# Row scatters, gate columns and one small addition around the hand-over from attention to experts: which engine does what, and what waits for what

## The chip, the core and the metric

The kernel runs on one core of a Trainium2 chip. The metric is the device time of one execution in microseconds (us). The core has a matrix engine (TensorE, PE in the rows; PEld are its weight loads), a vector engine (VectorE, DVE), a scalar engine (ScalarE, ACT), GpSimd (POOL) and a queue engine (SyncE, SP). Each runs its own list of instructions in order, and they wait for each other by semaphores. Indirect DMAs (gathers and scatters by row number) are issued by POOL.

## What is computed

Chunked attention (8 batches, 8 heads, 576 positions, chunks of 64), and behind it a mixture of experts on its 4608 output rows: each row goes to the one expert of 8 with the largest logit.

```python
attn = softmax(q_c @ k_c^T / 8)          # per chunk of 64
x = (attn @ v_c) as rows [4608, 512]
logits = x @ w_gate                      # [4608, 8]
gate = max softmax probability (sum + 1e-9); e = argmax
out[row] = gate * (relu(x @ w1[e]) @ w2[e])
```

## The kernel before

The 4608 rows are 36 tiles of 128. The main loop (L1067 on) takes two tiles at a time, 18 rounds `g`: PE makes the scores of round `g` (L251) into the PSUM pair `psS`, DVE takes the maxima and differences (`mx` L266, `ex` L269), ACT the exponentials (L274), PE transposes (L297) and multiplies with v (L306), DVE writes the normalised rows into a ring of blocks `xb` of four tiles each (L318), PE transposes the rows (L329) and forms the logits (L341). The scores of the next round go into the same `psS`, so PE has to wait there until DVE's `ex` of the round before has read it.

The rows are routed in batches of 6, 6, 6, 6, 4, 4, 2, 2 tiles (called batches 0 to 7 below) by a generator `route`, whose steps are dealt out between the steps of the rounds by hand: `small_op(n)` deals n DVE steps, `advance("a")` an ACT step, and so on. The whole order on PE, DVE, ACT and POOL is written out this way. The steps of `route` that matter here: `gs` is the sum of the exponentials (L411), 1e-9 is added to it (L413), its reciprocal is the gate in column 0 of the small tile `ft` (L415), column 1 of `ft` is the row's number (written by POOL, L362); `di` is the row's place in the sorted order (L424); POOL then copies the two columns of `ft` into columns 512 and 513 of the rows in `xb` (L426). `lo` (L386) is one of the small DVE steps before these, with both of its inputs in SBUF.

`store(n)` (L442) then issues the indirect scatters of n tiles from `xb` to the DRAM table `xd`, one for each tile, on POOL. With `after` given, ACT first copies a value into a spare column of the tile (L445, a "mark"), so that the scatter can't be issued before the thing it was copied from exists. Expert slot 0 needs the first 18 tiles alone (`TE[0]` is 18): `gather(0)` fetches its 256 rows from `xd` after those are stored, on POOL (L600), in the middle of the main loop. Later scatters write to the same table, and waited for these two gathers.

While the last rounds run, ACT splits the first expert's weights into a high part (`whi`, casts L89), and POOL subtracts for the low part (`wlo`, TENSOR_TENSOR L90, 16 of them, both inputs in SBUF).

After the loop comes the hand-over ("the tail" below, L1114 to L1187): PE transposes slot 0's rows (L625), ACT and DVE split them into `xhl` (L627, L628), and PE fills the rest with pieces of slot 0's matrix products (`filler`, L674 and L767 to L769), while the last batches are routed and stored; then DVE computes the tables of places, and `gather(1)` fetches slot 1's rows, once every scatter has landed. From there on PE runs one expert slot after the other until the end.

Of the kernel before, what the change touches and what calls it, by code (L numbers as in the profile page):

```python
# [8 lines left out]
F32 = mybir.dt.float32  # L9
# [3 lines left out]
AF = mybir.ActivationFunctionType  # L13
ALU = mybir.AluOpType
# [4 lines left out]
P = 128  # L19
NT = 4608  # L20
D = 512
# [5 lines left out]
RB = 4  # L27
# [3 lines left out]
NMAX = max(BATCHES)  # L31
# [19 lines left out]
def attn_moe_kernel(ctx: ExitStack, tc: tile.TileContext, q, k, v, wg, w, w0, out):  # L51
    nc = tc.nc
# [7 lines left out]
    q, k, v = (a[:, :, 0:G * D].rearrange("g p (i x) -> g p i x", i=G) for a in (q, k, v))  # L60
# [70 lines left out]
    sm = c1.enter_context(tc.tile_pool(name="sm", bufs=2))  # L131
# [28 lines left out]
    TE = [first[i] for i in EARLY]  # L160
# [185 lines left out]
    def route(b, pl):  # L346


        t0, n = first[b], BATCHES[b]
        S3 = [P, n, E]  # L350

        xts = [(i, G, xb[(t0 + i) // RB % XB], (t0 + i) % RB) for i in range(0, n, G)]
        vec = nc.vector

        def small(name, dt=F32, k=E):
            return sm.tile([P, NMAX, k], dt, name=name, bufs=2)[:, 0:n, :]

        def flat(x):
            return x.rearrange("p t o -> p (t o)")

        ft = sm.tile([P, NMAX, 2], F32, name="ft", bufs=2)[:, 0:n, :]
        nc.gpsimd.tensor_copy(ft[:, :, 1:2], pid[:, t0:t0 + n].unsqueeze(2))  # L362
        yield "c"
        lg = small("lg")
# [45 lines left out]
        gs = small("gs", k=1)  # L410
        vec.tensor_reduce(flat(gs), eg, AX.X, ALU.add)  # L411
        yield "v"
        vec.tensor_scalar(gs, gs, 1e-9, None, ALU.add)  # L413
        yield "v"
        vec.reciprocal(ft[:, :, 0:1], gs)  # L415
        yield "v"
# [5 lines left out]
        di = small("di", I32, 1)  # L422
        with nc.allow_low_precision("whole numbers"):
            vec.tensor_reduce(flat(di), dst, AX.X, ALU.add)  # L424
        for i, m, x, r in xts:
            nc.gpsimd.tensor_copy(x[:, r:r + m, D:D + 2], ft[:, i:i + m, :])  # L426
        waiting.extend((b, i, t0 + i, di) for i in range(n))
        yield "a"
# [2 lines left out]
        if b + 1 in EARLY:  # L431
            g = early(EARLY.index(b + 1))
            active.append([g, next(g), True])
        if b == NBAT - 1:
            g = tables()
            active.append([g, next(g), True])

    waiting = []

    def store(n, after=None):  # L440

        for k, (b, i, t, di) in enumerate(waiting[:n]):  # L442
            x = xb[t // RB % XB][:, t % RB, :]
            if k == 0 and after is not None:
                nc.scalar.copy(x[:, XW - 1:XW], after)  # L445
            stored.add(t)
            nc.gpsimd.indirect_dma_start(  # L447
                out=xds[b % 2 * NMAX + i],
                out_offset=bass.IndirectOffsetOnAxis(ap=di[:, i, :], axis=0),
                in_=x, in_offset=None, bounds_check=NT - 1, oob_is_err=False)  # L450
        del waiting[:n]

    active = []
# [133 lines left out]
    def rows_of(u):  # L587
        return xg[0] if u in (0, 2) else xg[1]
# [8 lines left out]

    def rows_in(t, u, h):
        rows = TE[u] * P if u < 2 and h < 2 else NT
        nc.gpsimd.indirect_dma_start(  # L600
            out=t[:, :], out_offset=None, in_=xd[0:rows, :],
            in_offset=bass.IndirectOffsetOnAxis(ap=place(u, h)[0:t.shape[0], :], axis=0),
            bounds_check=rows - 1, oob_is_err=False)

    def gather(u):
        for h in range(2):
            rows_in(rows_of(u)[h], u, h)

    def gather_x(u):
        rows_in(xg3, u, 2)  # L610
# [104 lines left out]
    lo_, h0 = [], []  # L715
# [305 lines left out]
    st_e, st_l, st_x = {}, {}, {}  # L1021
# [92 lines left out]
    g = NG - 1  # L1114
# [19 lines left out]
    for h in range(2):  # L1134
        ids(0, rows_of(0)[h], h)

    store(2, px[0][:, 0:1])
    filler(2)
    ri = soft_d(su)
    x_out(g, px, ri, xb[g * G // RB % XB])  # L1140
    logits(g - 1)
    store(2, st_l[g - 1][:, 0:1])
    filler(1)
    advance("t")
    small_op(5)
    advance("a")
    filler(1)
    st_x[g] = x_t(g, xb[g * G // RB % XB])
    store(2, st_x[g][:, 0, 0:1])
    sel_(g - 1)  # L1150
    advance("c")
    filler(2)
# [1 line left out]
    small_op(7)  # L1154
    advance("a")
    logits(g)
    store(2, st_l[g][:, 0:1])
    filler(1)
    advance("t")
    sel_(g)  # L1160
# [2 lines left out]
    advance("a")  # L1163
    pauses()
    filler(2)
    store(2, h0[-1][0][:, 0:1].bitcast(F32))
    pauses()
    small_op(7)
    advance("a")
# [6 lines left out]
    while active:  # L1176
        for x in "cat":
            advance(x)
        small_op(2)
        pauses()  # L1180
        side_op(3)
        if halves[0] > 5:
            filler(1)
        if h0:
            store(2, h0[-1][0][:, 0:1].bitcast(F32))
    store(NMAX)
    assert len(stored) == NTILE  # L1187
    gather(1)
# [204 lines left out]
```

## Time and profile before

| | us |
|---|---|
| median of 3 runs (range) | 573.17 (572.85 to 578.56) |
| the profiled execution | 576.16 |
| its span, first to last instruction | 574.3 |
| PE busy in it | 556.0 |
| DVE busy in it | 426.1 |

The profiled execution is one of the same kernel, 3.0 us above the median. Where stretches are named below, they are us from the start of its span: the main loop runs to about 114, the tail to about 150, the expert slots to the end.

### The profile page before, as it was taken

To read this page: it belongs to the slowest core of one execution; us is meant where nothing else is said; L and a number is where in the kernel's file an instruction comes from. 1 tells how busy PE (TensorE), PEld (TensorE's weight loads), DVE (VectorE), ACT (ScalarE), POOL (GpSimd) and SP (SyncE) were. 2 spreads that over 40 slices of the span, in tenths; PEclk is the share of its full clock that TensorE was granted. 3 is DMA by queue.
4 is the path that set the end of the run, shared out by engine and by line. 5 is a ranking of instruction groups with operands and counts; after the bars stand their busy time and mean duration, and the time that the engine had idled before them with its cause. 6 is when DMAs were issued, how large, how long until landed. Compare 5 with 4: busy or idle time off the path is not lost.

```text
span 574.3 us, 13260 instructions
## 1 busy us (share of the span) xinstructions
PE 556.0 (97%) x4858; PEld 489.8 (85%) x4858; DVE 426.1 (74%) x840; ACT 281.8 (49%) x548; POOL 270.3 (47%) x293
## 2 busy tenths in 40 slices
PE   7999999979999999999999999999998999999995
PEld 6788888878898888999898898888988888899894
DVE  8899999976695878776787588645665765588775
ACT  1667766743244464554654454424443542356553
POOL 6025743387643655525473574523514252274352
PEclk9999999989999999999999999999998999999998
DMA  8999999435584453456145636644622652232021
GB/s 267 406 394 352 370 356 365 156 143 199 158 323 141 142 189 91 139 190 215 47 144 166 205 93 207 227 139 136 210 63 82 203 178 94 60 104 80 19 62 38
DMA packets 49038, 102.70 MB, mean 179 GB/s; under 512 B 14176, under 2 KB 28512, under 8 KB 45312
## 3 DMA queue, kind: packets, MB, share of 16 engines
q0 software_dynamic: 19776, 61.14, 31.2%
q1 hardware_dynamic: 29120, 39.88, 20.6%
q8 instruction: 63, 1.03, 0.8%
q14 instruction: 79, 0.65, 0.4%
HBM read 113.75 MB, written 19.56 MB: 232 GB/s over the span
## 4 chain that ended last, share of the span: by engine, by line
PE 57%; issue 10%; DMA 6%; POOL 3%; DVE 2%; POOLq 0%; ACT 0%; DVEq 0%
PE psS L674 11%; PE psS L681 11%; DMA xg<-xd,idx 5%; PE psV L767 4%; PE psV L769 4%; PE psV L768 4%; PE psU L769 4%; PE psU L768 4%; PE psU L767 4%; PE psL L681 3%; PE psL L674 3%; POOL xg L600 1%; POOL raw L573 1%; PE psK L785 1%; PE psK L787 1%
## 5 line engine op out<-in xcount | busy, mean ns | idle before, releaser
L83 DVE TENSOR_TENSOR wlo<-raw,whi 128x1024 fp32r<-128x1024 f32 x118 | 142.3, 1216 | 17.7 <-ACT whi L82 17.4
L82 ACT CAST whi<-raw 128x1024 fp32r<-128x1024 f32 x118 | 121.9, 1046 | 2.8 <-DMA raw<-in_w,widx 2.8
L701 ACT ACTIVATE hh<-psS 128x256 fp32r<-128x256 f32 x98 | 37.7, 384 | 158.0 <-PE psS L674 83.1
L573 POOL DMA_INDIRECT raw<-in_w,widx x62 | 70.0, 1129 | 93.9 <-DVE wlo L83 63.7
L799 POOL DMA_INDIRECT out_y<-y,oid x40 | 51.7, 1293 | 110.0 <-issue 28.3
L674 PE MATMUL psS<-xhl,whi 128*128 128x256 f32 x496 | 93.6, 288 | 3.2 <-DVE xhl L628 2.9
L600 POOL DMA_INDIRECT xg<-xd,idx x68 | 79.8, 1173 | 27.3 <-issue 17.3
L674 PEld LDWEIGHTS psS<-xhl,whi 128*128 128x128 f32 x496 | 81.4, 195 | 7.6 <-issue 4.2
L706 DVE SCALAR_TENSOR_TENSOR hl<-psS,hh 128x256 fp32r<-128x256 f32 x98 | 41.1, 421 | 59.2 <-ACT xx L685 37.8
L674 PE MATMUL psS<-xhl,wlo 128*128 128x256 f32 x248 | 71.1, 286 | 0.0
L681 PE MATMUL psS<-xhl,whi 128*128 128x320 f32 (+2 forms) x288 | 59.8, 333 | 0.5 <-ACT xhl L665 0.5
L681 PEld LDWEIGHTS psS<-xhl,whi 128*128 128x128 f32 x288 | 49.6, 188 | 4.6 <-ACT xhl L665 0.6
L767 PE MATMUL psV<-whi,hh 128*128 128x512 f32 x128 | 51.1, 399 | 2.3 <-issue 2.3
L769 PE MATMUL psU<-whi,hl 128*128 128x512 f32 x128 | 50.2, 392 | 0.3 <-DVE hl L706 0.3
L767 PE MATMUL psU<-whi,hh 128*128 128x512 f32 x128 | 50.4, 394 | 0.0
L768 PE MATMUL psU<-wlo,hh 128*128 128x512 f32 x128 | 50.4, 393 | 0.0
L768 PE MATMUL psV<-wlo,hh 128*128 128x512 f32 x128 | 50.1, 391 | 0.0
L769 PE MATMUL psV<-whi,hl 128*128 128x512 f32 x128 | 50.1, 391 | 0.0
L674 PEld LDWEIGHTS psS<-xhl,wlo 128*128 128x128 f32 x248 | 48.4, 195 | 0.0
L447 POOL DMA_INDIRECT xd<-xb,di x32 | 31.6, 988 | 17.4 <-issue 10.6
L90 POOL TENSOR_TENSOR wlo<-raw,whi 128x512 fp32r<-128x512 f32 x16 | 20.2, 1276 | 40.9 <-DMA spare<-in_k 23.8
L767 PEld LDWEIGHTS psV<-whi,hh 128*128 128x128 f32 x128 | 24.1, 188 | 8.6 <-issue 3.1
(257 smaller groups left out, 1151.7 us busy)
## 6 DMA issues: line engine op xcount, KB each, us to landing
qt<-in_q SPq DMA_DIRECT2D x17, 512.0 KB
xg<-xg SPq DMA_DIRECT2D x224, 32.0 KB
vb<-in_v SPq DMA_DIRECT2D x12, 512.0 KB
kb<-in_k SPq DMA_DIRECT2D x22, 256.0 KB
raw<-in_w SPq DMA_DIRECT2D x16, 256.0 KB
spare<-in_k SPq DMA_DIRECT2D x12, 256.0 KB
spare<-in_v SPq DMA_DIRECT2D x6, 512.0 KB
xg<-xd,idx POOLq DMA_INDIRECT x68, 3.6
```

The costliest lines, as they stand in the source:

```text
L82: nc.scalar.copy(hi, src)
L83: nc.vector.tensor_tensor(lo, src, hi.bitcast(F32), ALU.subtract)
L573: nc.gpsimd.indirect_dma_start(out=raw[c][:, :], out_offset=None, in_=w, in_offset=bass.IndirectOffsetOnAxis(ap=widx[:, u, c:c + 1], axis= ...
L600: nc.gpsimd.indirect_dma_start(out=t[:, :], out_offset=None, in_=xd[0:rows, :], in_offset=bass.IndirectOffsetOnAxis(ap=place(u, h)[0:t.sha ...
L674: nc.tensor.matmul(ph, a, b[:, kc, 0:BLK], start=kc + i == 0, stop=kc + i == 5)
L681: nc.tensor.matmul(ph, a[par][kc][:, f * 128:(f + 1) * 128], b[:, kc, 0:BLK + n], start=kc + i == 0, stop=kc + i == 5)
L701: nc.scalar.activation(hh, ph, AF.Relu)
L706: nc.vector.scalar_tensor_tensor(hl, ph, 0.0, hh.bitcast(F32), ALU.max, ALU.subtract)
L767: nc.tensor.matmul(py, hh, wh, start=f == 0, stop=False)
L768: nc.tensor.matmul(py, hh, wl, start=False, stop=False)
L769: nc.tensor.matmul(py, hl, wh, start=False, stop=f == 7)
L799: nc.gpsimd.indirect_dma_start(out=outs[m], out_offset=bass.IndirectOffsetOnAxis(ap=oid[u % 3][0:n, m:m + 1], axis=0), in_=y, in_offset=No ...
```

## The change

Five edits, which belong to the same part of the program. Below the changed lines the line numbers rise, by 4 to 8 (L413 becomes L417 and L628 becomes L636).

1. The row numbers `di` get four buffers in place of two.
2. Batches whose tiles lie in one block of `xb` (batches 4 to 7) have no `ft`: POOL writes the row number, and DVE the gate, straight into the rows; the copies by POOL (L426) fall away for them.
3. The addition of 1e-9 to `gs` moves from DVE (TENSOR_SCALAR) to ACT (an ACTIVATE with a bias), for all eight batches.
4. Scatters of tiles from 18 on are declared independent of slot 0's two gathers.
5. The stores of the tail have no mark any more.

```diff
         def small(name, dt=F32, k=E):
-            return sm.tile([P, NMAX, k], dt, name=name, bufs=2)[:, 0:n, :]
+            return sm.tile([P, NMAX, k], dt, name=name, bufs=4 if name == "di" else 2)[:, 0:n, :]
...
-        ft = sm.tile([P, NMAX, 2], F32, name="ft", bufs=2)[:, 0:n, :]
+        whole = t0 % RB + n <= RB
+        if whole:
+            ft = xts[0][2][:, t0 % RB:t0 % RB + n, D:D + 2]
+        else:
+            ft = sm.tile([P, NMAX, 2], F32, name="ft", bufs=2)[:, 0:n, :]
         nc.gpsimd.tensor_copy(ft[:, :, 1:2], pid[:, t0:t0 + n].unsqueeze(2))
...
-        vec.tensor_scalar(gs, gs, 1e-9, None, ALU.add)
+        nc.scalar.activation(flat(gs), flat(gs), AF.Copy, bias=1e-9)
         yield "v"
         vec.reciprocal(ft[:, :, 0:1], gs)
...
-        for i, m, x, r in xts:
+        for i, m, x, r in () if whole else xts:
             nc.gpsimd.tensor_copy(x[:, r:r + m, D:D + 2], ft[:, i:i + m, :])
...
-            nc.gpsimd.indirect_dma_start(
+            put = nc.gpsimd.indirect_dma_start(
...
+            if t >= TE[0]:
+                for got in fetched:
+                    tc.declare_no_dep(put.ins, got.ins, reason="rows from TE[0] * P on, and rows in front of them")
...
     def gather(u):
-        for h in range(2):
-            rows_in(rows_of(u)[h], u, h)
+        got = [rows_in(rows_of(u)[h], u, h) for h in range(2)]
+        if u == 0:
+            fetched.extend(got)
...
-    store(2, px[0][:, 0:1])
+    store(2)
...
-    store(2, st_x[g][:, 0, 0:1])
+    store(2)
...
-        if h0:
-            store(2, h0[-1][0][:, 0:1].bitcast(F32))
+        store(2)
```

(Three more stores of the tail lose their mark in the same way.)

On ACT in the main loop, at batch 1 (the batch whose `gs` DVE sums at 64.66 in the profile), the list read, with what each row waits for in brackets:

```order
L274 ACTIVATE ex<-ex 128x1024 [waits DVE_49]
L89 CAST whi_4_73<-raw_67 128x512 [waits DMAHW3_49]
L89 CAST whi_4_73<-raw_67 128x512 [waits DMAHW4_49]
L1040 COPY lp<-psL 128x256 [waits PE_49]
L429 ACTIVATE cb<-psK 128x8 [waits DVE_49]
```

and it reads now:

```order
L274 ACTIVATE ex<-ex 128x1024 [waits DVE_49]
L89 CAST whi_4_73<-raw_67 128x512 [waits DMAHW3_49]
L89 CAST whi_4_73<-raw_67 128x512 [waits DMAHW4_49]
L417 ACTIVATE gs<-gs 128x6 [waits DVE_49]
L1048 COPY lp<-psL 128x256 [waits PE_49]
L433 ACTIVATE cb<-psK 128x8 [waits DVE_49]
```

The addition stands behind the round's exponentials and behind two weight casts. At batch 0 it stands behind one cast, at batch 2 behind none, at batch 3 behind one, and each time behind the exponentials. DVE has nothing between `gs` and the reciprocal in these four batches, so its reciprocal waits for this row.

On DVE at the start of the tail (batch 4), before:

```order
L411 TENSOR_REDUCE gs<-eg 128x4
L413 TENSOR_SCALAR gs<-gs 128x4 [waits DVE_49]
L628 TENSOR_TENSOR xhl<-psS,xhl 128x4x128 [waits DMAHW6_49,DMAHW7_49,DMAHW5_49,Activation_49]
L628 TENSOR_TENSOR xhl<-psS,xhl 128x4x128 [waits Activation_49]
L415 RECIPROCAL ft<-gs 128x4 [waits DVE_49,Pool_49]
L419 TENSOR_TENSOR dst<-psK,oh_b 128x32
L424 TENSOR_REDUCE di<-dst 128x4 [waits DMASW6_49,DMASW1_49,DMASW7_49,DMASW0_49,DVE_49]
```

and now:

```order
L415 TENSOR_REDUCE gs<-eg 128x4
L636 TENSOR_TENSOR xhl<-psS,xhl 128x4x128 [waits DMAHW6_49,DMAHW7_49,DMAHW5_49,Activation_49]
L636 TENSOR_TENSOR xhl<-psS,xhl 128x4x128 [waits Activation_49]
L419 RECIPROCAL xb_124<-gs 128x4
L423 TENSOR_TENSOR dst<-psK,oh_b 128x32
L428 TENSOR_REDUCE di<-dst 128x4 [waits DVE_49]
```

The addition is gone from in front of the two `xhl` rows, for which PE waits (on ACT it stands in front of the two casts of `xhl`), and `di` waits for no scatter (DMASW) any more.

On POOL around slot 0's gathers, before:

```order
L600 DMA xg_64<-xd,idx_260 128x528 [waits PE_49]
L426 COPY xg_64<-ft 128x2x2 [waits DVE_49,Pool_49]
L426 COPY xb_123<-ft 128x2x2 x2
L447 DMA xd<-xg_64,di 4608x528 [waits DMASW2_49,DVE_49,DMASW3_49,Activation_49,Pool_49]
L447 DMA xd<-xg_64,di 4608x528
L362 COPY ft<-pid 128x4
L90 TENSOR_TENSOR wlo_6_83<-raw_68,whi_6_75 128x512 [waits DMAHW0_49,Activation_49]
L90 TENSOR_TENSOR wlo_7_84<-raw_68,whi_7_76 128x512 [waits DMAHW1_49,Activation_49]
```

and now:

```order
L607 DMA xg_64<-xd,idx_260 128x528 [waits PE_49]
L430 COPY xg_64<-ft 128x2x2 [waits DVE_49,Pool_49]
L430 COPY xb_123<-ft 128x2x2 x2
L451 DMA xd<-xg_64,di 4608x528 [waits DVE_49,Activation_49,Pool_49]
L451 DMA xd<-xg_64,di 4608x528
L366 COPY xb_124<-pid 128x4
L90 TENSOR_TENSOR wlo_6_83<-raw_68,whi_6_75 128x512 [waits DMAHW0_49,Activation_49]
L90 TENSOR_TENSOR wlo_7_84<-raw_68,whi_7_76 128x512 [waits DMAHW1_49,Activation_49]
```

The order is the same; the scatter behind the gathers no longer waits for their landing (DMASW2 and DMASW3).

## Rows read from the trace of the kernel before

**Rows 1.** The page, part 1: busy us, share of the span, instructions.
```profile
PE 556.0 (97%) x4858; PEld 489.8 (85%) x4858; DVE 426.1 (74%) x840; ACT 281.8 (49%) x548; POOL 270.3 (47%) x293
```
**Rows 2.** Busy time by stretch: stretch and length; busy of each engine; clock, DMA.
```profile
0.00:20.00 20.00, 15.22 (x235) 13.31 (x236) 17.27 (x28) 5.66 (x8) 8.98 (x45) 1.00 0.88 308
46.40:116.00 69.60, 69.35 (x1416) 59.15 (x1410) 65.78 (x127) 50.07 (x120) 36.25 (x47) 1.00 0.87 312
117.00:120.00 3.00, 0.18 (x2) 0.00 (x0) 3.00 (x3) 1.07 (x3) 2.83 (x3) 1.00 0.23 90
120.00:124.00 4.00, 3.88 (x43) 3.49 (x47) 3.33 (x16) 1.30 (x5) 3.09 (x4) 0.57 0.49 188
```
**Rows 3.** What PE waited for, whole span: us in total, times, longest.
```profile
PE psS L674 <- DVE xhl L628: 2.9, 1, 2.9
...
PE psS L251 <- DVE ex L269: 1.2, 1, 1.2
...
PE psQ L625 <- DMA xg<-xd,idx: 0.5, 1, 0.5
```
**Rows 4.** DVE in order of time, tail: start, us, row [idle before].
```profile
115.85 0.17 DVE L411 TENSOR_REDUCE gs<-eg 128x4 f32<-128x32 f32 x1
116.06 3.16 DVE L413 TENSOR_SCALAR gs<-gs 128x4 f32<-128x4 f32 x1
119.13 1.28 DVE L628 TENSOR_TENSOR xhl<-psS,xhl 128x512 fp32r<-128x512 f32 x2
...
138.28 0.17 DVE L424 TENSOR_REDUCE di<-dst 128x2 int32<-128x16 f32 x1 [1.20 <-issue]
```
**Rows 5.** POOL in order of time, four places.
```profile
40.95 1.27 POOL L90 TENSOR_TENSOR wlo<-raw,whi 128x512 fp32r<-128x512 f32 x1 [4.61 <-DMA spare<-in_k]
...
114.19 1.05 POOL L447 DMA_INDIRECT xd<-xg,di  x1 [5.01 <-ACT whi L89]
...
116.67 2.51 POOL L90 TENSOR_TENSOR wlo<-raw,whi 128x512 fp32r<-128x512 f32 x2
...
145.32 1.04 POOL L600 DMA_INDIRECT xg<-xd,idx  x1 [3.41 <-DVE kb L921]
```
**Rows 6.** ACT in order of time, start of the tail.
```profile
115.94 0.58 ACT L627 CAST xhl<-psS 128x512 fp32r<-128x512 f32 x1
...
116.48 0.61 ACT L627 CAST xhl<-psS 128x512 fp32r<-128x512 f32 x1
```
**Rows 7.** DVE in order of time, main loop (batches 0 and 1).
```profile
41.31 0.98 DVE L386 TENSOR_TENSOR lo<-am,iota_m 128x48 bf16<-128x48 f32 x1
...
64.66 0.19 DVE L411 TENSOR_REDUCE gs<-eg 128x6 f32<-128x48 f32 x1
...
65.09 0.19 DVE L415 RECIPROCAL ft<-gs 128x6 f32<-128x6 f32 x1
...
69.47 1.23 DVE L269 TENSOR_TENSOR ex<-psS,mx 128x1024 f32<-128x1024 f32 x1
```
**Rows 8.** ACT in order of time, main loop (the same round).
```profile
63.90 0.23 ACT L284 ACTIVATE su<-su 128x16 f32<-128x16 f32 x1
64.77 1.06 ACT L274 ACTIVATE ex<-ex 128x1024 f32<-128x1024 f32 x1 [0.64 <-DVE ex L269]
65.74 1.12 ACT L89 CAST whi<-raw 128x512 fp32r<-128x512 f32 x2
66.77 0.36 ACT L1040 COPY lp<-psL 128x256 f32<-128x256 f32 x1
```
**Rows 9.** What DVE waited for between 46.4 and 116.0: us, times, longest.
```profile
DVE ri L289 <- ACT su L284: 0.4, 2, 0.3
DVE mx L266 <- ACT xb L445: 0.2, 1, 0.2
DVE xg L318 <- PE psV L306: 0.2, 1, 0.2
```
**Rows 10.** PE's weight loads in order of time: the round's scores.
```profile
71.34 1.73 PEld L251 LDWEIGHTS psS<-spare,qt 128*64 128x64 f32 x32 [0.41 <-DVE ri L289]
```

More of the change, by code (lines that the diff above doesn't have):

```diff
@@ L436, in route @@
             active.append([g, next(g), True])
-    waiting = []
+    waiting, fetched = [], []
     def store(n, after=None):
@@ L599, in rows_in @@
         rows = TE[u] * P if u < 2 and h < 2 else NT
-        nc.gpsimd.indirect_dma_start(
+        return nc.gpsimd.indirect_dma_start(
             out=t[:, :], out_offset=None, in_=xd[0:rows, :],
@@ L1141, in attn_moe_kernel @@
     logits(g - 1)
-    store(2, st_l[g - 1][:, 0:1])
+    store(2)
     filler(1)
@@ L1156, in attn_moe_kernel @@
     logits(g)
-    store(2, st_l[g][:, 0:1])
+    store(2)
     filler(1)
@@ L1165, in attn_moe_kernel @@
     filler(2)
-    store(2, h0[-1][0][:, 0:1].bitcast(F32))
+    store(2)
     pauses()
@@ L1183, in attn_moe_kernel @@
             filler(1)
-        if h0:
-            store(2, h0[-1][0][:, 0:1].bitcast(F32))
+        store(2)
     store(NMAX)
```

## The prediction, made before the changed kernel had run

> **What bounds the kernel now.** I began with the page's busy shares: PE is busy for 556.0 of 574.3 us [rows 1], so an edit pays only where it shortens one of PE's few gaps, and costs only where it opens one. The list of PE's waits then shows which gaps are near the change [rows 3]: 2.9 us at the start of the tail, where the first product of slot 0 waits for DVE's `xhl`, and 0.5 us at the end of the tail, where slot 1's transposes wait for gathered rows.
>
> The first is the one to read closely. By the stretches [rows 2], PE does 0.18 us of work between 117 and 120, and from 120 to 124 its granted clock is 0.57 on the mean (partly 1.2, partly 2.4 GHz), where it had been 1.00 until then. So the gap costs twice: 2.9 us of waiting, and behind it 4.0 x (1 - 0.57) = 1.7 us of lost speed.
>
> Why is `xhl` late? In DVE's order of time [rows 4] the addition of 1e-9 to four numbers per partition begins at 116.06 and takes 3.16 us; at batch 1 the whole step from `gs` to the reciprocal, this addition included, takes 65.09 - 64.66 = 0.43 us [rows 7]. It ends at 119.22, and POOL's two `wlo` subtractions run from 116.67 to 119.18 [rows 5]. The addition is held up by POOL, and both `xhl` steps stand behind it, though ACT had cast both halves by 116.48 + 0.61 = 117.09 [rows 6].
>
> The Trainium skill, page "SBUF — State Buffer", section "Who interferes with whom", says that VectorE and GpSimd share one pair of SBUF ports as an exclusive lock held for a whole instruction, and that `tensor_scalar` is one of the operations that can ask for both ports. The trace agrees as to the blocking (3.16 us, ending 0.04 us behind POOL's pair).
>
> The main loop is the other place. PE is busy for 69.35 of 69.60 us there [rows 2], and DVE, with 65.78, waits for others 0.8 us in all [rows 9]; the rest of its idle time is the few hundredths between neighbours (127 instructions). Both engines are full, and tied to each other: PE's scores at 71.34 need `psS`, which DVE's `ex` leaves at 69.47 + 1.23 = 70.70 [rows 7, 10]. PE has 0.64 us in hand there, no more.
>
> **The change, part by part.**
>
> *The addition moved to ACT, in the tail (batch 4).* On DVE the 3.16 us go. On ACT the addition now stands in front of the casts of `xhl`. `gs` is ready at 115.85 + 0.17 = 116.02 [rows 4], and ACT's first cast stood at 115.94 [rows 6]; so the casts move by about 0.2 us (the nearest ACT row, the same Copy with a bias for `su`, lasts 0.23 [rows 8]). The first half is then cast at 115.94 + 0.2 + 0.58 = 116.72, and DVE's first `xhl` starts at about 116.75 in place of 119.13: 2.4 us earlier. PE's wait shrinks from 2.9 to about 0.5, and I expect the clock to hold, which is worth the 1.7: the start of the kernel has a PE wait of 1.2 us in a stretch at clock 1.00 [rows 2, 3]. Bounds for the clock: 0 and 1.7. Tail gain so far: -2.4 - 1.7 = -4.1.
>
> *The same move in the main loop (batches 0 to 3).* Here the addition cost DVE little, and the move adds a wait: the reciprocal, with all of DVE behind it, now waits for ACT, whose list has the exponentials and the weight casts ahead of the addition. At batch 1, from rows 8: exponentials at 64.77, two casts from 65.74, the addition at 66.77 where `lp` stood, 0.23 long; reciprocal at about 67.0 in place of 65.09. That is 1.9 us of DVE. Each cast is (66.77 - 65.74) / 2 = 0.5, so one cast gives 1.4, none 0.9. With one, two, none and one cast (the order of ACT): 1.4 + 1.9 + 0.9 + 1.4 = 5.6 us. What hides it? DVE can catch up only where it waits for others now, 0.8 us [rows 9]. Behind DVE's stall stand the places `di`, the normalised rows (L318) for which PE's transposes wait, and the next `ex`, for which the next scores wait, with the 0.64 us in hand at batch 1. PE soon uses up what it has in hand, and then runs behind DVE. So 5.6 - 0.8 = 4.8 us reach the tail. Bounds: 0 (if the rounds have more play than the rows show) and 5.6.
>
> *Scatters freed from slot 0's gathers.* POOL's first scatter behind the gathers sat idle for 5.01 us, to 114.19 [rows 5]. Without that wait POOL's whole backlog of the tail comes forward. PE does not wait for these scatters themselves. A side effect: the two `wlo` subtractions behind them come forward too, to near where DVE has batch 4's routing, `lo` among it. `lo` with both inputs in SBUF took 0.98 us at 41.31, and ended as POOL's subtraction of 40.95 did (42.22) [rows 5, 7]; a small step nearby, `gs` at 64.66, takes 0.19. Price: 0 if they miss each other, at most 1.27 for one subtraction; I take 0.4, a third of it, since the two may meet only in part.
>
> *The gates straight into the rows, four buffers of `di`, no marks.* These take six POOL copies and six ACT copies out, and a wait of 1.20 us in front of the last `di` [rows 4]. All of it leads to the last scatters and so to `gather(1)`, which POOL issued at 145.32 after 3.41 us of idling [rows 5], and for which PE waited 0.5 us [rows 3]. With POOL's backlog gone, the last batch's scatters follow their `di` at once. I expect the gather early enough also for a PE that arrives 4.1 us sooner: two scatters of about 1 us follow a `di` that is itself 4.1 + 1.2 us earlier. Gain 0.5 (bounds 0 and 0.5, since PE has nothing else to win there; were the gather not to keep pace, up to 4.1 would be given back, which is a rival below).
>
> *Sum against the profiled execution.* 4.8 + 0.4 - 2.4 - 1.7 - 0.5 = +0.6 us, so 576.16 + 0.6 = 576.8. That execution was 2.99 us above the median, so in terms of the median 573.17 + 0.6 = 573.8. About 1% is what a measurement of this kernel can tell from no change: 5.7 us, 567.4 to 578.9.
>
> **The rivals.**
>
> *The main loop's stalls are hidden.* If PE and DVE have play that the rows don't show, only the tail counts: -2.4 - 1.7 - 0.5 = -4.6, so 568.6. Against it: DVE's 0.8 us of waits in 69.6, and the scores 0.64 us behind `ex` [rows 9, 10]. For it: only some of DVE's small steps are needed by PE at once. Chance 0.22, with parts of it in between; in 0.05 something more is gained and the time falls under 567.4.
>
> *Slower: the clock falls in the main loop too.* The stalls of batches 0, 1 and 3 reach PE as waits of up to about 1.3 us (1.9 - 0.64 at batch 1). A wait of 2.9 us lowered the clock, one of 1.2 did not [rows 2, 3]. If the limit lies below 1.3 us, each of three waits costs another 1.7, and the tail's 1.7 is not won back, since its remaining wait follows closely: 573.8 + 3 x 1.7 + 1.7 = 580.6. Chance 0.05.
>
> *The tail's gain is given back.* Another DVE step takes the addition's place behind POOL's subtractions (the Trainium skill, in the section named above, says that two-input steps in SBUF, as `lo` is, meet GpSimd's reads at the same port; the 0.98 us of `lo` agree), or `gather(1)` doesn't come forward, and PE waits there what it won. By the row of `lo` one collision more costs up to 1.27; by the gather up to 4.1. Then 573.8 + 1.3 to 573.8 + 4.1, that is 575.1 to 577.9. Chance 0.17.
>
> *The change does not do what it says.* If the addition on DVE was not what held `xhl`, PE's 2.9 us stay, and the main loop's cost stands alone: 573.17 + 5.2 = 578.4. Chance 0.04, since the end of the addition and the start of `xhl` (119.22 and 119.13 [rows 4]) leave no room for another cause.
>
> **How the numbers follow.** My own sum has 0.52, with a range of its own of about 571.5 to 576 (clock and `lo` at their bounds). Predicted: 573.8. The range reaches down to the hidden stalls (568.6) and up to a tail gain given back (578.0). Faster by over 1%: 0.05. Slower by over 1%: 0.06, the clock rival and a piece of the last one. Within: 0.89.
>
> **What the changed profile would show.** In the tail, no DVE row of 3 us, `xhl` right behind ACT's casts, a PE wait below 1 us and clock 1.00 behind it. In the main loop, DVE idle for 0.9 to 1.9 us before each of the first four reciprocals with ACT as the releaser, PE waiting before scores in the rounds of batches 1 and 3, and the tail's first step on DVE, `gs` at 115.85 [rows 4], some 5 us later. At the end of the tail no wait of PE for gathered rows. The prediction is wrong if those waits on ACT are there and PE does not wait, or if the clock drops in the loop.

## The result, and the profile after

The changed kernel takes 575.47 us (median of 22 executions, 573.53 to 581.17), the kernel before 572.2 us beside it (22 executions, 568.74 to 578.56). The ratio is 1.0052, with a 95% interval of 1.0031 to 1.0073, so by the ratio the change costs 3.0 us (1.8 to 4.2). Forecast were 573.8 us and +0.6 us, with a range of 568.6 to 578.0. The time lies in the range and the change is within 1%, as expected; the difference, though, is five times the forecast one, and the experiments show that only half of the argument was right. They also met chips on which the change costs nearly three times as much, for a reason of which the forecast had no word.

The profiled execution of the changed kernel took 576.14 us, that of the kernel before 576.16. First what PE waited for, over the whole span (us in total, times, longest):

```profile
PE psS L251 <- DVE ex L269: 4.3, 4, 1.5
...
PE psT L671 <- DMA out_y<-y,oid: 1.5, 1, 1.5
...
PE psS L682 <- ACT at L298: 0.9, 1, 0.9
...
PE psS L633 <- PE psL L341: 0.4, 1, 0.4
```

Against [rows 3], the first product of slot 0 (now L682) waits 0.9 us in place of 2.9, and the profile names ACT's copies of `at` as what ended that wait, no longer DVE's `xhl`. The 0.5 for gathered rows are gone. The scores (L251) wait 4.3 us for DVE's `ex`, in four places, where it was 1.2 in one; that one, at the start of the kernel, is still among the four, and the other three, 3.0 us, lie in the main loop. The stretches (length; busy time of PE, PEld, DVE, ACT, POOL; clock, DMA share, GB/s) say the same:

```profile
46.40:116.00 69.60, 66.09 (x1321) 55.86 (x1320) 61.06 (x119) 47.93 (x118) 39.43 (x51) 1.00 0.90 319
117.00:120.00 3.00, 2.57 (x55) 2.05 (x46) 2.87 (x6) 1.77 (x3) 2.11 (x3) 1.00 0.46 180
120.00:124.00 4.00, 3.11 (x32) 2.60 (x34) 3.08 (x10) 2.66 (x10) 3.02 (x4) 1.00 0.36 139
```

In [rows 2] PE was busy for 69.35 us of the main loop's 69.60 and DVE for 65.78; now it is 66.09 and 61.06. In the tail the hole between 117 and 120 is filled, and the clock stays at 1.00 where it was 0.57. The first is the cost of the change, the second its gain in this pair. DVE in order of time, the reciprocals of the first four batches:

```profile
47.45 0.19 DVE L419 RECIPROCAL ft<-gs 128x6 f32<-128x6 f32 x1 [1.63 <-ACT gs L417]
...
67.19 0.19 DVE L419 RECIPROCAL ft<-gs 128x6 f32<-128x6 f32 x1 [2.15 <-ACT gs L417]
...
85.71 0.19 DVE L419 RECIPROCAL ft<-gs 128x6 f32<-128x6 f32 x1 [1.18 <-ACT gs L417]
...
105.56 0.19 DVE L419 RECIPROCAL ft<-gs 128x6 f32<-128x6 f32 x1 [1.70 <-ACT gs L417]
```

The bracket is the idle time ahead of the instruction and who ended it. These waits contain the place of the addition that DVE no longer does (about 0.2 us); less that they are 1.4, 1.9, 1.0 and 1.5, where 1.4, 1.9, 0.9 and 1.4 were forecast. The tail on DVE and on ACT, against [rows 4, 6]:

```profile
119.83 0.17 DVE L415 TENSOR_REDUCE gs<-eg 128x4 f32<-128x32 f32 x1
120.82 1.29 DVE L636 TENSOR_TENSOR xhl<-psS,xhl 128x512 fp32r<-128x512 f32 x2 [0.81 <-ACT xhl L635]
```
```profile
120.04 0.20 ACT L417 ACTIVATE gs<-gs 128x4 f32<-128x4 f32 x1 [0.57 <-DVE gs L415]
120.20 0.59 ACT L635 CAST xhl<-psS 128x512 fp32r<-128x512 f32 x1
```

No addition of 3 us stands on DVE. `xhl` starts 0.99 us behind `gs` (before: 119.13 - 115.85 = 3.28), and ACT has the addition of 0.20 us ahead of its cast. The tail itself starts 4 us later (`gs` at 119.83 for 115.85). POOL and the two places on DVE where the scatters matter:

```profile
110.44 1.05 POOL L451 DMA_INDIRECT xd<-xg,di  x1 [0.16 <-POOL xb L430]
...
113.32 2.50 POOL L90 TENSOR_TENSOR wlo<-raw,whi 128x512 fp32r<-128x512 f32 x2 [0.32 <-ACT whi L89]
...
143.24 1.04 POOL L607 DMA_INDIRECT xg<-xd,idx  x1 [2.57 <-DVE tot L912]
```
```profile
114.16 0.48 DVE L390 TENSOR_TENSOR lo<-am,iota_m 128x32 bf16<-128x32 f32 x1
...
137.50 0.17 DVE L428 TENSOR_REDUCE di<-dst 128x2 int32<-128x16 f32 x1
```

Against [rows 5], the first freed scatter follows POOL's copies after 0.16 us in place of 5.01, and `gather(1)` is issued 2.1 us earlier. `lo` does meet POOL's `wlo` and takes 0.48 us, and the last `di` has lost its wait of 1.20 [rows 4].

Both programs give PE the same 4858 instructions in the same order, so the starts of one and the same product can be set side by side (us from the start of the span):

| product | before | after | after later by |
|---|---|---|---|
| first of the block of L306 ahead of batch 0's `gs` | 44.91 | 44.57 | -0.34 |
| first of the last block of L306 but one | 112.91 | 116.31 | 3.40 |
| first of L663 (now L671), behind the tail | 152.53 | 151.95 | -0.58 |
| L767 (now L775) at 428 | 428.21 | 428.34 | 0.13 |
| L767 (now L775) at 446 | 446.35 | 444.46 | -1.89 |
| L767 (now L775) at 565 | 564.68 | 563.37 | -1.31 |

So the main loop costs PE 3.7 us, and the tail gives 4.0 back. What follows, in the expert slots, has little to do with the change. Above all the kernel before has a second stretch at half clock there, of 3.4 us, behind a wait of 2.3 us at L767 (marked as issue). The changed kernel has the same wait with 1.8 us, and the clock stays at 1.00 behind it. First before, then after:

```profile
434.20:437.50 3.30, 3.30 (x17) 3.22 (x16) 0.75 (x1) 0.36 (x2) 2.42 (x3) 0.50 0.46 152
```
```profile
434.20:437.50 3.30, 3.30 (x29) 3.30 (x29) 1.68 (x3) 1.95 (x4) 2.57 (x3) 1.00 0.52 182
```

So in this pair of profiles each step is where the forecast put it, and the two executions are equal within 0.02 us. But the medians are 3.0 us apart. The execution of before that was profiled lay 4 us above its median; that of after, less than 1 us. What made it so was the first question.

### The profile page after: what moved, and what is told of

It reads as the page before. It is cut to its first block, busy times and chain, and to the rows that moved or that the text cites. A ratio compares the mean times of both kernels' runs of the same rounds, so it can differ in the third digit from the quotient of the medians.

```text
span 574.3 us, 13236 instructions
## 1 busy us (share of the span) xinstructions
PE 554.0 (96%) x4858; PEld 487.7 (85%) x4858; DVE 421.1 (73%) x832; ACT 282.6 (49%) x550; POOL 270.7 (47%) x287
## 4 chain that ended last, share of the span: by engine, by line
PE 58%; issue 10%; DMA 6%; POOL 3%; DVE 2%; POOLq 1%; ACT 1%; DVEq 0%; ACTq 0%
PE psS L682 11%; PE psS L689 10%; DMA xg<-xd,idx 5%; PE psV L775 4%; PE psV L776 4%; PE psV L777 4%; PE psU L777 4%; PE psU L776 4%; PE psU L775 4%; PE psL L689 3%; PE psL L682 3%; POOL xg L607 1%; POOL raw L580 1%; PE psK L793 1%; PE psK L795 1%
## 5 line engine op out<-in xcount | busy, mean ns | idle before, releaser
L580 POOL DMA_INDIRECT raw<-in_w,widx x62 | 71.7, 1156 | 90.5 <-DVE wlo L83 61.6
L682 PE MATMUL psS<-xhl,whi 128*128 128x256 f32 x496 | 91.8, 284 | 1.8 <-PE psV L777 0.9
L682 PEld LDWEIGHTS psS<-xhl,whi 128*128 128x128 f32 x496 | 79.7, 191 | 6.3 <-issue 1.7
L682 PE MATMUL psS<-xhl,wlo 128*128 128x256 f32 x248 | 70.2, 283 | 0.0
L689 PEld LDWEIGHTS psS<-xhl,whi 128*128 128x128 f32 x288 | 49.6, 188 | 4.6 <-ACT xhl L673 0.6
L775 PE MATMUL psV<-whi,hh 128*128 128x512 f32 x128 | 51.1, 400 | 1.8 <-issue 1.8
L775 PE MATMUL psU<-whi,hh 128*128 128x512 f32 x128 | 50.4, 394 | 0.0
L682 PEld LDWEIGHTS psS<-xhl,wlo 128*128 128x128 f32 x248 | 47.4, 191 | 0.0
L775 PEld LDWEIGHTS psV<-whi,hh 128*128 128x128 f32 x128 | 24.0, 188 | 8.0 <-issue 2.6
```

The costliest lines, as they stand in the source:

```text
L580: nc.gpsimd.indirect_dma_start(out=raw[c][:, :], out_offset=None, in_=w, in_offset=bass.IndirectOffsetOnAxis(ap=widx[:, u, c:c + 1], axis= ...
L682: nc.tensor.matmul(ph, a, b[:, kc, 0:BLK], start=kc + i == 0, stop=kc + i == 5)
L689: nc.tensor.matmul(ph, a[par][kc][:, f * 128:(f + 1) * 128], b[:, kc, 0:BLK + n], start=kc + i == 0, stop=kc + i == 5)
L775: nc.tensor.matmul(py, hh, wh, start=f == 0, stop=False)
```

## The experiments

Each was timed against the kernel before on the same chip, in the same rounds. They fell on four chips, and these are of two kinds. On one, the kernel before took 572.51 us, as at first (572.2): the first kind below. On three others it took 583.57, 584.98 and 582.77: the second kind. Each of the four was met once, so whether the kind goes with the chip for good isn't told. Ratios are therefore compared within a kind. In the diffs `-` is the kernel that the heading names.

### The kernel before once more

No edit.

> The kernel before, once more, for a second trace of it. Theory A (clock): the half-speed stretch of TensorE behind the 2.9 us wait at the start of the tail is not in every execution; the profiled one, 3 to 4 us above the median, had it, a usual one has not. Then a trace near the median shows the same 2.9 us wait for xhl and the clock at 1.00 from 120 to 124. Theory B (rest of the program): the drop is in every execution, and what the changed kernel lost against the forecast (+3.0 us measured, +0.6 forecast) lies in the expert slots. Then the clock is near 0.57 there again. Time: 1.000 of before either way.

Measured, second kind: 582.94 us, ratio 0.9981 (0.9956 to 1.0007). The tail's addition, that of [rows 4] which took 3.16 us, is here:

```profile
123.17 0.17 DVE L413 TENSOR_SCALAR gs<-gs 128x4 f32<-128x4 f32 x1
```

It takes 0.17 us in the same program, for POOL's pair of `wlo` (from 120.62, 2.54 us) was over just as it began, and PE has no wait of 2.9 us. So the stall comes with executions in which POOL's `wlo` falls on the addition, and not with every execution of the kernel. How often it comes on the first kind isn't told by this trace, whose main loop is stretched as told below; a run further down bears on it.

### The addition on ScalarE, and nothing else (before)

```
-        vec.tensor_scalar(gs, gs, 1e-9, None, ALU.add)
+        nc.scalar.activation(flat(gs), flat(gs), AF.Copy, bias=1e-9)
```

> The kernel before with the one edit that the addition of 1e-9 goes to ScalarE, for all batches. Both theories see VectorE idle for about 1.6, 2.1, 1.2 and 1.7 us before the first four reciprocals, as in the changed kernel, and about 4.2 us of that reach TensorE by the tail; the wait for xhl shrinks by 2.4 us; the 0.5 us wait for slot 1's rows stays. Theory A: +4.2 - 2.4 = +1.8 us, and more (about +2.3) if other small collisions stay. Theory B: +4.2 - 2.4 - 1.7 = +0.1 us. A third one, C: the other four edits cost something; then this one alone is nearer to 0 than the full change's +3.0.

Measured, second kind: 584.38 us, ratio 1.0017 (0.9988 to 1.0047). DVE's waits for the additions are there (8.4 us in seven), but PE waits for `ex` only 1.2 us, once, as in the kernel before. On this kind of chip it stands for other reasons, told below; that what DVE loses is hidden behind these is argued, not shown.

### The addition back on VectorE (after), for all batches or the first four

```
-        nc.scalar.activation(flat(gs), flat(gs), AF.Copy, bias=1e-9)
+        vec.tensor_scalar(gs, gs, 1e-9, None, ALU.add)
```

> The changed kernel with the addition back on VectorE, for all batches: the other four edits alone. All theories see the four waits of the main loop gone. In the tail GpSimd's two wlo subtractions come some 4 us earlier than in the kernel before (the scatter in front of them waits for no gather), so they end before the addition of batch 4 begins at about 116: it takes 0.2 to 1.3 us in place of 3.16. Theory A: -2.4 - 0.5 = about -2.9 us against before (0.995). Theory B: -4.6 us (0.992). Theory C: 0 or slower. If the wlo pair meets the addition all the same, the time is within 0.5 us of before.

The second puts it on VectorE for `b < 4` and leaves it on ScalarE for the rest.

> The changed kernel with the addition on VectorE for batches 0 to 3 and on ScalarE for batches 4 to 7. The main loop's four waits are gone, the tail is that of the changed kernel. Theory A: -2.4 - 0.5 = about -2.9 us against before (0.995), and about 5 us under the changed kernel. Theory B: -4.6 us (0.992). Theory C: slower than before.

Measured, second kind: 592.15 us, ratio 1.0137 (1.0105 to 1.0169), and 592.21, ratio 1.0135 (1.0105 to 1.0165). Two of the three theories expected both to be faster than the kernel before, and both are 8 us slower, as only the third had it, for which the other four edits cost something. The waits of the main loop are gone, so on these chips the loss lies elsewhere. PE's list of waits names it. First the kernel before on this kind, then the changed kernel (from the next run):

```profile
PE psV L306 <- issue: 3.1, 6, 1.0
...
PE psU L306 <- issue: 1.6, 4, 0.5
```
```profile
PE psU L306 <- issue: 5.1, 13, 0.5
PE psV L306 <- issue: 4.3, 11, 0.5
```

L306 is attention times values, a block of 64 small products of 64x64. On the first kind of chip these rows don't exist in any of the five traces. From the timelines, the length of each block follows (start of its first product to the end of its last). Until POOL's first scatter, at about 50 us, all blocks take 1.16 to 1.19 us on both kinds. From then on the kernel before has blocks of 1.16 to 1.25 us on the first kind, and of 1.21 to 2.53 on the second: 9.5 us over 1.16 in twelve blocks, nearly the 11 us between the two kinds. The three last blocks of the kernels run on the second kind, with the later runs among them, in us:

```
kernel                        last three blocks      ratio to before
before once more               1.56  1.21  2.53      0.9981
before, no marks               1.20  1.16  2.18      0.9983
before, addition on ScalarE    1.43  1.17  1.87      1.0017
before, scatters moved         1.16  1.16  1.50      1.0017
after                          4.17  2.34  5.68      1.0147
after, addition on VectorE     3.55  2.90  5.46      1.0137
the same, beside after         4.51  2.98  5.70      1.0139
after, on VectorE for b < 4    3.82  2.98  5.60      1.0135
after, without the addition    3.55  1.66  5.62      1.0122
```

Every kernel with the four other edits has 5.5 to 7.9 us more in these three blocks than the kernel before once more. The theory formed on the first of these runs: on these chips a scatter that POOL issues while PE is in such a block stops PE.

### The changed kernel on the second kind

No edit.

> The changed kernel as it is, beside the kernel before on one chip. Theory S (scatters meet attention): in the trace of the kernel before on the second chip, every block of 64 matmuls of line 306 that had one of POOL's row scatters beside it took 1.56 to 2.53 us (one: 1.56 to 2.53 with idle PE marked as issue), the blocks ahead of the first scatter 1.16 to 1.19; on the first chip all took 1.16. With the addition on VectorE again the changed order had three tail blocks of 3.55, 2.90 and 5.46 us where the kernel before has 1.56, 1.21 and 2.53: 6.6 us. If this is such a chip, the changed kernel is slower than before by 6 to 9 us (ratio 1.010 to 1.016); if it is one like the first, all blocks take 1.16 us and the difference is 2 to 4 us. Theory C (clock drops): the profiled execution of before at first held two drops of 3.4 us at half clock, 1.7 us each, which usual executions do not have; without them after is 2.3 us slower on either chip (ratio 1.004).

Measured: 593.57 us, ratio 1.0147 (1.0095 to 1.0198), so 8.6 us where the first kind showed 3.0. POOL in order of time beside its last block, and PE's first and stopped products of that block:

```profile
134.65 0.99 POOL L451 DMA_INDIRECT xd<-xb,di  x1 [4.76 <-issue]
135.95 0.98 POOL L451 DMA_INDIRECT xd<-xb,di  x1 [0.30 <-issue]
137.24 0.98 POOL L451 DMA_INDIRECT xd<-xb,di  x1 [0.30 <-issue]
138.52 0.99 POOL L451 DMA_INDIRECT xd<-xb,di  x1 [0.30 <-issue]
```
```profile
135.22 0.27 PE L306 MATMUL psU<-vb,at 64*64 64x64 f32 x1
...
136.71 0.21 PE L306 MATMUL psU<-vb,at 64*64 64x64 f32 x1 [0.48 <-issue]
...
137.47 0.25 PE L306 MATMUL psV<-vb,at 64*64 64x64 f32 x1 [0.47 <-issue]
...
138.19 0.26 PE L306 MATMUL psU<-vb,at 64*64 64x64 f32 x1 [0.44 <-issue]
...
138.93 0.25 PE L306 MATMUL psV<-vb,at 64*64 64x64 f32 x1 [0.39 <-issue]
...
139.66 0.21 PE L306 MATMUL psV<-vb,at 64*64 64x64 f32 x1 [0.41 <-issue]
...
140.37 0.36 PE L306 MATMUL psU<-vb,at 64*64 64x64 f32 x1 [0.49 <-issue]
```

Four scatters in a row cover the block. Of its 64 products 41 go through before the first stop; from then on PE gets a few done every 0.7 us, waiting for nothing that the profile shows. In the changed kernel on the first kind scatters lie on blocks just so (at 115.98 and 117.28, beside the block of 116.31), and that block takes 1.16 us.

The clock has a share in the loss as well. Behind these stops it fell to half (1.2 GHz) for 3.4 us; first the stretch with the stops, then that at half clock:

```profile
135.20:140.00 4.80, 2.49 (x57) 1.59 (x56) 1.31 (x10) 1.30 (x6) 3.40 (x4) 1.00 0.43 169
140.10:143.30 3.20, 2.93 (x19) 2.82 (x20) 0.37 (x2) 0.38 (x1) 0.00 (x0) 0.50 0.20 78
```

Over the executions, the five runs on this kind with the four other edits have a median clock of 0.989 to 0.990, the kernel before beside them 0.994 to 0.996. By an estimate (the difference times 590 us) that is worth 2.4 to 3.8 us. With the longer blocks it comes to more than the whole loss, so a little is won elsewhere.

### The addition on VectorE, beside it

The same edit as above.

> The changed kernel with the addition of line 417 on VectorE again, beside the changed kernel itself on the same chip. Theory S: on a chip whose blocks of line 306 are stretched by scatters, about 592/583.6 of before (ratio 1.014) as measured at first, and within 3 us of the changed kernel: the scatters' places decide, not the addition. On a chip whose blocks all take 1.16 us: the 4.8 us of ScalarE waits in the main loop are gone, the 2.9 us wait of the tail is back, so 1.5 to 3 us faster than the changed kernel. Rival (the addition itself costs it on VectorE): slower than the changed kernel by 5 us or more on either chip.

Measured: 592.37 us, ratio 1.0139 (1.0084 to 1.0193). As on the chip before; the addition's place is worth about 1 us on this kind, less than the interval.

### The kernel before without the marks of the tail

```
-    store(2, px[0][:, 0:1])
+    store(2)
...
-        if h0:
-            store(2, h0[-1][0][:, 0:1].bitcast(F32))
+        store(2)
```

All six marked calls behind the loop are changed so.

> The kernel before with only the marks taken out of the tail: its scatters are no longer held until a result of PE or ScalarE is there. Theory S: on a chip with stretched blocks the scatters of the last two batches start earlier and lie on the last two or three blocks of line 306, 4 to 7 us more than before (ratio 1.007 to 1.012); on a chip with blocks of 1.16 us no change (0 to -1 us). Rival (the loss comes from the scatters freed of slot 0's gathers): no change on either chip.

Measured, second kind: 583.98 us, ratio 0.9983 (0.9954 to 1.0012). My theory had expected 4 to 7 us more. The marks alone hold nothing: while the scatters behind the gathers wait for these (the first at 118.84, after 2.93 us of idling), the ones behind them are late without any mark, and the blocks stay short. The theory's mechanism stands, its assignment to the marks alone does not.

### The main loop's scatters moved from the scores to the block

```
-        store(2, ps[:, 0, 0:1])
...
             px = attn_v(ga, at)
+            store(2, px[0][:, 0:1])
```

> The kernel before with one line moved: in the main loop the two scatters are held by a mark on the attention output of the block just issued, not on the scores ahead of it, so that they start when a block of line 306 ends and are done before the next (two scatters take 2.4 us, the period is 7). Theory S: on a chip with stretched blocks ten blocks of 1.8 to 2.3 us go to 1.2 us, 6 to 9 us faster than before (ratio 0.985 to 0.990); on a chip with blocks of 1.16 us nothing changes, within 1 us. Rival (the stretch is PE's own supply of instructions, whatever POOL does): the blocks stay at 1.8 to 2.3 us, within 1 us of before on either chip.

Measured, second kind: 586.62 us, ratio 1.0017 (0.9985 to 1.0049); expected were 6 to 9 us less. Yet this run shows, by an edit, that the scatter's place decides. Six blocks, at 89 to 123 us, now have no scatter beside them (before: one), and five still have. The six took 1.16 or 1.17 us, the five 1.66 to 3.09. The first and the last product of one of the six:

```profile
89.17 0.27 PE L306 MATMUL psU<-vb,at 64*64 64x64 f32 x1
...
90.11 0.22 PE L306 MATMUL psV<-vb,at 64*64 64x64 f32 x1
```

Over all nine traces from the second kind, 65 blocks have none of POOL's scatters or gathers within them; 64 of these are within 0.05 us of 1.16, and one, with a scatter that ended 0.3 us ahead of it, took 1.50. The other 97 take 0.27 to 4.53 us more, about 1.3 us for each us of overlap (correlation 0.98; in part this follows of itself, since a longer block meets more scatters). What was won in the blocks went into waits of PE, above all for ScalarE's copies of `at` (0.3 us in the kernel before on this kind), less for `kb` (1.6 there); why these came late was not followed up:

```profile
PE psT L329 <- ACT at L298: 4.7, 6, 1.2
PE psS L251 <- DMA kb<-in_k: 2.5, 2, 1.4
```

### The scatters freed of the gathers, alone and without the marks (before)

```
+            if t >= TE[0]:
+                for got in fetched:
+                    tc.declare_no_dep(put.ins, got.ins, reason="rows from TE[0] * P on, and rows in front of them")
```

> The kernel before with one edit alone: later tiles' scatters no longer wait for slot 0's gathers; all marks stay. Theory S (a scatter beside a block of line 306 stops PE for 0.6 to 0.7 us at a time on chips of the second kind): the two scatters that wait 3 to 5 us at the end of the main loop start about 4 us earlier and fall on the block at about 114 us, which goes from 1.2 to 1.6 us to 3 to 4 us; the blocks after it stay under 2.6 us, since their scatters are still held by the marks. So 2 to 4 us slower than before on such a chip (ratio 1.003 to 1.007), and no change on a chip whose blocks all take 1.16 us. Rival (this edit carries the whole loss): ratio 1.013 to 1.016, with all three last blocks stretched. Rival (it carries none): 1.000, the block at 114 us unchanged.

The second has this and the dropped marks.

> The kernel before with two edits: later tiles' scatters freed of slot 0's gathers, and the marks out of the tail; the addition stays on VectorE and the rows and buffers as before. Without the freed scatters the marks alone were worth nothing (0.9983). Theory S: together the two put scatters on all three last blocks of line 306 (3 to 4.5, 2.3 to 3, and 5 to 6 us, as in the changed kernel), 6 to 9 us slower than before on a chip of the second kind (ratio 1.010 to 1.016), no change on one of the first. Rival (the rows and buffers are needed for the loss): under 1.007.

Measured, on a chip of the first kind: 573.33 us, ratio 0.9998 (0.9970 to 1.0027), and 571.92, ratio 0.9976 (0.9946 to 1.0007). Neither costs anything there, as the theory has it for this kind; whether they cost what it says on the second was not told by these runs. The trace of the first again has the addition on DVE, in the tail of a first-kind chip:

```profile
118.60 0.17 DVE L413 TENSOR_SCALAR gs<-gs 128x4 f32<-128x4 f32 x1
119.08 1.29 DVE L632 TENSOR_TENSOR xhl<-psS,xhl 128x512 fp32r<-128x512 f32 x2 [0.32 <-ACT xhl L631]
```

With the scatters freed, POOL's `wlo` stood at 113.74 and was over by then. The addition has no 3 us to give, and moving it would win nothing. It also tells of the kernel before: had its usual execution on this kind the stall and the half clock behind it (4.1 us by the forecast), a kernel without them would be faster by as much. It is not, by more than the 1.7 us of the interval, unless freeing the scatters costs elsewhere what this gives. In the second trace the collision sits elsewhere, on `lo`, which starts just ahead of POOL's pair (110.94, 2.52 us) and ends with it; the addition meets a later one in part:

```profile
110.86 2.66 DVE L386 TENSOR_TENSOR lo<-am,iota_m 128x32 bf16<-128x32 f32 x1
```
```profile
118.92 0.91 DVE L413 TENSOR_SCALAR gs<-gs 128x4 f32<-128x4 f32 x1
```

### The scatters between two blocks

```
-        store(2, ps[:, 0, 0:1])
...
-        cast(g)
+        if ga < 0:
+            cast(g)
...
             x_out(ga, px, ri, xb[ga * G // RB % XB])
+            store(2, px[0][:, 0:1], nc.vector.tensor_copy)
+            cast(g)
```

VectorE writes the mark here.

> The kernel before with the main loop's scatters put between two blocks of line 306: held by a mark that VectorE writes behind x_out (no ScalarE copy, so ScalarE waits for nothing new), and ahead of POOL's wlo of that round, since the casts now stand behind x_out too. With the mark on ScalarE and POOL's wlo ahead of the scatters, the blocks with no scatter beside them took 1.16 us and five others still 1.7 to 3.1, and PE waited 4.7 us for ScalarE's copies of at instead. Theory S: eleven blocks go from 1.6 to 2.3 us to 1.2 us; 5 to 9 us faster than before on a chip of the second kind (ratio 0.985 to 0.992) if nothing new waits, no change on one of the first. Rival (PE's stops move elsewhere, it is its supply of instructions on average that bounds): blocks of 1.2 us but the same time, ratio 0.998 to 1.004, with new waits of PE marked as issue at other lines. Rival (the casts come too late): waits for whi or raw, slower.

Measured, first kind: 578.4 us, ratio 1.0099 (1.0062 to 1.0136). All blocks take 1.16 to 1.20 us, but on this kind they did before. The cost shows on DVE. POOL's `wlo`, now behind the scatters, begins about when DVE has its small steps of routing, and these take 2 us for 0.2; PE waits for the `ex` behind them:

```profile
56.91 1.99 DVE L371 TENSOR_TENSOR lg<-lg,lm 128x48 f32<-128x48 f32 x1
...
65.26 1.61 DVE L413 TENSOR_SCALAR gs<-gs 128x6 f32<-128x6 f32 x1
```
```profile
PE psS L251 <- DVE ex L269: 4.7, 6, 1.2
```

Whether it pays on the second kind stays untried. None of the versions tried beats the kernel before on either kind by more than its interval.

### The changed kernel without the addition

```
-        nc.scalar.activation(flat(gs), flat(gs), AF.Copy, bias=1e-9)
```

> The changed kernel with the addition of 1e-9 left out (neither VectorE nor ScalarE adds it; a part of the computation, whose sums are 1 or more), so that the reciprocal follows the sum on VectorE with no turn to ScalarE. On a chip of the first kind (blocks of line 306 of 1.16 us), theory R (the turn to ScalarE is the whole loss, the freed scatters and dropped marks cost nothing there, as 0.9998 and 0.9976 said): the four waits of 1.2 to 2.2 us ahead of the reciprocals go, 4 to 5 us faster than the changed kernel, so 0.995 to 0.999 of the kernel before. Rival (the rows written straight and the further buffers cost the 3 us): it stays at 1.003 to 1.007. On a chip of the second kind theory S: the three last blocks stay stretched, 1.010 to 1.016 whatever becomes of the addition; a ratio under 1.005 there would refute it.

Measured, second kind: 589.8 us, ratio 1.0122 (1.0079 to 1.0164). Without any addition, on either engine, two of the three last blocks stay stretched (3.55, 1.66, 5.62 us) and the loss stays. What the turn to ScalarE costs on the first kind would have been told by this run there; on this chip it could not be.

## Why the prediction was right, and where it was not

*Main loop, +4.8: the mechanism seen in the trace, the size a little too large.* The waits came at the four reciprocals and within 0.1 us of their forecast sizes. PE's waits for `ex` rose by the 3.0 us in the main loop, and the tail started 4.0 us later on DVE; PE's own products fell behind by 3.7 (0.5, 1.3, 0.2 and 1.6 us at the four batches). So about 2 us of the waits were hidden, where the forecast allowed 0.8. The two edits on the scatters together gave 0.9976 on the first kind, all edits 1.0052; the quotient, 1.0076, leaves about 4.4 us (2.2 to 6.5 by the two intervals) to the addition on ScalarE, the rows and the buffers. The addition was not separated from the rows and buffers by a run on this kind, so that it alone costs this is argued from the waits in the trace.

*Tail, -4.1: the step that failed.* "On DVE the 3.16 us go" was read off the one execution at hand, and there it was true: PE won 4.0 us in the tail of this pair. What failed is to take it as a gain of the median. The addition took 0.17 us in the same kernel in its second trace (second kind), 0.17 with the scatters freed alone, and 0.91 with the marks gone too (first kind); and 0.9998 for the freed scatters leaves at most 1.7 us of such a gain in the usual execution of before, if freeing costs nothing elsewhere. That the time lies in the range all the same is in part luck: of the 4.1 us that were missing, 1.7 were made up by terms that cost less than forecast, the main loop and the scatters. The stall is a meeting of two instructions, and the other edits of the same change pull POOL's `wlo` forward (to 113.32, from 116.67), off the addition. So the gain was claimed for an edit that had nothing left to win beside them.

*The clock, -1.7 of these: mis-sized as well.* The profiled execution of before held the drop behind the tail's wait and a second one at 434 us, and its mean clock was 0.991. Of the 23 other executions of before on the first kind, the six with a mean clock of 0.998 or more have spans with a median of 569.5 us, the five at 0.994 or less, 572.7. So the drops are a matter of the execution (3.2 us go along with them there), and the one profiled was among the disturbed ones. Setting the sum against its own time and then carrying the difference over to the median took over a gain that at least these six executions already had; for the others no trace tells. Without the 4.1 the forecast would have been +0.6 + 4.1 = +4.7, and with the measured -1.4 of the scatters (an interval that holds zero) in place of the -0.1 that I gave them, 4.8 - 1.4 = +3.4. Measured: +3.0. This sum was made after the result and is no test.

*Scatters and `lo`, +0.4:* 0.48 us where `lo` without POOL takes about 0.2, so 0.3 in this trace, where it ended in the middle of POOL's pair of two subtractions; 2.5 in another, where it ended only with the whole pair. My bound of 1.27, for one subtraction, was too low.

*Gather, -0.5:* as forecast, PE no longer waits for gathered rows. Further on it waits 0.9 us more for a scatter of outputs (1.5 for 0.6); whether the one follows from the other was not looked into.

*The rivals.* That the clock falls in the loop did not happen, with waits of up to 1.5 us at clock 1.00. That the stalls are hidden fell on the first kind; on the second it came near the truth (1.0017 with the addition alone on ScalarE): the waits on ACT are there and PE does not wait, which the forecast had named as its sign of being wrong. That the change does not do what it says fell too: `xhl` follows `gs` after 0.99 us. That the tail's gain is given back came out in its time (575.1 to 577.9) by another way: in the median little of that gain was there to give back. No rival had scatters that stop PE. "PE does not wait for these scatters themselves" is true by semaphores and on the first kind, and false on the second, where the blocks and the clock make up the loss; on the first kind's trace, with blocks of 1.16 to 1.25 us, no row could have said so.

What stays open: why the chips differ, and what it is that stops PE, since the profile names no releaser for it. One rival is that PE's own instructions come late; 41 products ahead of the first stop would fit it, but in that block the trace has no packet of instructions under way from 135.6 us to the end. That freed scatters and dropped marks together, and not the rows and buffers, bring the three long blocks is read from the order of scatters in the traces; the run that would have shown it fell on the first kind.

## What to carry to other kernels

A stall in one profiled execution is a candidate, not yet a cost: before a gain is booked on it, look whether the two instructions that collide stand in a fixed order, and whether the execution is a usual one by its time and clock. A short step that is moved to another engine costs the wait for that engine's list, and if the engine it leaves is full and feeds PE, most of that arrives (here 3.7 of 5.8 us). Where a kernel holds transfers back by marks or dependencies, the hold may be what keeps them away from something; look at what runs beside the new place, and on more than one chip.

## What the runs showed of the hardware

On three of the chips, a block of 64 products of 64x64 took 1.16 us with none of POOL's row transfers beside it (64 of 65 blocks), and up to 5.70 us with four in a row; PE then went on about every 0.7 us for a few products. In the five traces of the first kind the same overlap cost less than 0.1 us. The same program thus took 572 us on some chips and 583 to 585 on others, 2% apart, which is more than any edit here brought.

An addition on 128x4 elements took from 0.17 to 3.16 us, and a comparison of 128x32 elements from 0.18 to 2.66, by where POOL's subtractions stood. The longest two began 0.6 and 0.1 us ahead of POOL's pair and still ended only with it; POOL was busy with a scatter or a copy of four columns when they began, so it isn't shown that they were first. Two other comparisons (128x32 and 128x48), begun while the first subtraction of a pair ran, ended between the two (0.48 us at 114.16 in the changed kernel, 0.84 at 60.14 in the kernel before).

Waits of PE of up to 1.5 us in the changed kernel's main loop left the granted clock at 1.00; behind one of 2.9 us and one of 2.3 us in the kernel before it fell to half for 3.4 us each, and behind one of 2.4 us in another trace (scatters freed, marks dropped) it stayed at 1.00.
